# A sigmoid written as a tanh, and a new issue order, in a kernel of attention and a gated feed-forward layer

## The chip, the core and the metric

The kernel runs on one core of a Trainium2 chip. The metric is the device time of one execution in microseconds (us); lower is better. The engines are named as the profile names them: PE multiplies matrices (PEld is its weight load), ACT evaluates functions and copies, DVE does elementwise work and sums, POOL helps DVE and issues some transfers, SP issues most transfers. On-chip data lie in SBUF, results of PE in banks of PSUM.

## The reference

```python
# attention: 8 batches, 8 heads, 576 tokens, head size 64; keys and values are averaged over groups of 8 tokens
scores = q @ k_pooled.T / sqrt(64);  attn = softmax(scores);  x = attn @ v_pooled     # x becomes 4608 x 512
gate = 1.0 / (1.0 + np.exp(-(x @ w_gate)))                                           # w_gate 512 x 1536
out  = (gate * (x @ w_val)) @ w_out                                                  # w_out 1536 x 512
```

Everything is in 32-bit floats. The softmax needs `exp`, the gate a sigmoid.

## The kernel before

The tokens are handled in nine blocks of 512. Block 0 goes through `first_pass`, together with the preparation of blocks 1 and 2; then come four rounds of two blocks each (`hidden`, which computes the hidden values, and `second_sums`, which multiplies them by `w_out`). In a round the attention of the next two blocks is computed piece by piece between the products of the feed-forward layer.

To keep 32-bit precision, each operand of the large products is split into a high and a low part, and a product is three matmuls (high by high, high by low, low by high). The high part is a CAST on ACT, the low part a subtraction on DVE (in `first_pass` now and then on POOL). The rounds use sums and differences of quarters of the matrices, so that seven products do the work of eight; `sG`, `sV`, `s`, `y` in the profile are such partial results. The weights arrive as 64-bit numbers and are converted in `to_f32` with a `Prelu` and a `Relu` on ACT; the converted parts are kept in DRAM and loaded again in each round.

Three places compute the gate: `gate`/`h_of` in `first_pass`, `gated` at the start of the first round, and the end of `product` in the rounds. Each takes a 128x512 result of PE, applies the sigmoid on ACT, and multiplies it on DVE by the matching result of `w_val`. There are 108 such pairs of instructions. `attention`, `exps` and `total` compute the softmax; its sums are multiplied by `POOL` = 8 before the reciprocal is taken, which divides by the group size too.

The order in which instructions stand on their engines is not that of the code. The code runs once with `book.open`, and every instruction becomes a numbered unit; some matmuls that belong together are one unit. The string `LATER` lists all these numbers, and at the end the units are issued in its order:

```python
    with tc.manual_schedule(engines={e.engine for e in engines}):
        for n in LATER.split() or range(len(book.units)):
            for taken in book.units[int(n)]:
                taken.issue(link)
```

Each engine then works through its own instructions strictly in this order, and waits where an operand or a buffer isn't ready. ACT holds one table of functions at a time: where `Exp` follows `Sigmoid` or the other way round, the build puts an ACT_TABLE_LOAD in between; `Prelu`, `Relu` and copies need none.

All instructions are recorded by one helper, so the profile shows L317 for nearly all of them (L312 in the change, which has five lines fewer); the rows are told apart by the names of the tiles. `chain` are results of x by `w_gate` or `w_val`, `acc` results of the hidden values by `w_out`, `sc` scores, `tp` and `tr` transposed probabilities, `av` the attention's result, `xo` and `hs` split operands that stream through PE, `parts` and `oparts` split weights, `h` and `early` the hidden values and small data of the first pass that lie in the same room.

Of the kernel before, what the change touches and what calls it, by code (L numbers as in the profile page):

```python
# [15 lines left out]
AF = mybir.ActivationFunctionType  # L16
ALU = mybir.AluOpType
# [4 lines left out]
POOL = 8  # L22
# [7 lines left out]
BT = 512  # L30
# [299 lines left out]
def attention_then_ffn(ctx: ExitStack, tc: tile.TileContext, qT, kT, vm, vr, vn, sums8, wgv, wo, const, out, outT):  # L330
# [530 lines left out]


    bank, seen, gates, hb = {}, {}, {}, {}

    def chain_bank(kind, b):
        return ps.tile([P, BT], F32, name="chain", tag=CHAIN["GV".index(kind) * 3 + "ABC".index(b)])

# [710 lines left out]
```

## Time and profile before

| | |
|---|---|
| time, median of 3 runs | 905.96 us (905.59 to 908.38) |
| span of the profiled execution | 904.9 us |
| PE busy | 893.7 us, 99% |
| DVE busy | 657.9 us, 73% |
| ACT busy | 544.4 us, 60% |
| POOL busy | 199.5 us, 22% |
| ACT_TABLE_LOAD after the first | 47.5 us in 37 instructions |
| granted PE clock | 0.999 of full speed |

The profiled execution is not one of the three timed ones, and no time of its own is given beside its span; the median of the timed runs lies 1.06 us above the span. A matmul of 512 columns is recorded with about 392 ns, but the next one starts before it ends, so the busy time of PE is the union of such rows. Idle time of PE is what a change can give back; idle time of the others only matters where PE waits for them.

### The profile page before, as it was taken

Reading aid. Unit: us, or ns where it says so; the run is one execution under the profiler, and the core shown is the slowest. Engines: PE = TensorE matmul, PEld = TensorE weight load, DVE = VectorE, ACT = ScalarE, POOL = GpSimd, SP = SyncE. Lnnn points to the kernel's source line nnn. Section 1 sums busy time; section 2 is a strip of 40 time slices with the busy share of each in tenths; the row PEclk is TensorE's granted clock in tenths of the full one; section 3 lists DMA queues with packets and bytes.
Section 4 is the critical chain, followed back from the end, with each engine's and each line's share of the span. In section 5 each row is a group of like instructions: output and inputs, shape, how many; then the busy total and the mean of one; then the engine's idle time right before and its main releaser. Section 6 shows DMA issues by size and latency. Waiting matters only on the chain.

```text
span 904.9 us, 12649 instructions
## 1 busy us (share of the span) xinstructions
PE 893.7 (99%) x4162; PEld 734.5 (81%) x4162; DVE 657.9 (73%) x1039; ACT 544.4 (60%) x1108; POOL 199.5 (22%) x369
## 2 busy tenths in 40 slices
PE   7999999999999999999999999999999999999998
PEld 6778888888888888888888888888888888888886
DVE  7989888889899999756668796355589552224863
ACT  5998998788978476545375555445365552224352
POOL 2411101012164235453443104132213000000000
PEclk9999999999999999999999999999999999999999
DMA  9899888889999888798987888776747775646653
GB/s 344 289 329 340 304 338 294 297 290 333 319 334 305 282 288 286 233 302 257 308 278 233 245 274 259 235 265 196 266 120 254 244 251 206 228 166 206 195 167 141
DMA packets 100289, 237.56 MB, mean 263 GB/s; under 512 B 13856, under 2 KB 34720, under 8 KB 98688
## 3 DMA queue, kind: packets, MB, share of 16 engines
q1 hardware_dynamic: 85040, 203.84, 66.7%
q0 software_dynamic: 15040, 32.79, 10.7%
q8 instruction: 33, 0.54, 0.2%
q14 instruction: 32, 0.26, 0.1%
q10 hardware_dynamic: 144, 0.13, 0.0%
HBM read 176.02 MB, written 60.69 MB: 262 GB/s over the span
## 4 chain that ended last, share of the span: by engine, by line
PE 81%; ACT 2%; DVE 2%; issue 0%; DVEq 0%
PE chain L317 50%; PE acc L317 25%; PE av L317 3%; PE sc L317 3%; ACT hs L317 0%; DVE s L317 0%; DVE hs L317 0%; PE tp L317 0%; DVE h L317 0%; ACT e L317 0%; ACT L317 0%; ACT raw_o L317 0%; DVE w_o L317 0%; ACT w_o L317 0%; ACT oparts L317 0%
## 5 line engine op out<-in xcount | busy, mean ns | idle before, releaser
L317 PE MATMUL chain<-xo,parts 128*128 128x512 f32 x2316 | 544.0, 392 | 0.2 <-ACT xs L317 0.2
L317 PEld LDWEIGHTS chain<-xo,parts 128*128 128x128 f32 x2316 | 430.6, 188 | 93.0 <-issue 1.0
L317 PE MATMUL acc<-hs,oparts 128*128 128x512 f32 x1008 | 237.0, 391 | 0.3 <-issue 0.2
L317 PEld LDWEIGHTS acc<-hs,oparts 128*128 128x128 f32 x1008 | 188.1, 188 | 40.6 <-DVE hs L317 1.2
L317 POOL DMA_DIRECT2D turned<-turn x240 | 131.7, 551 | 215.9 <-DVE turn L317 184.4
L317 DVE TENSOR_TENSOR y<-chain,sV 128x512 f32<-128x512 f32 x46 | 31.2, 687 | 70.4 <-PE chain L317 54.7
L317 DVE TENSOR_TENSOR hs<-h,hs 128x1024 fp32r<-128x1024 f32 x52 | 63.0, 1218 | 10.5 <-ACT hs L317 10.3
L317 ACT CAST hs<-h 128x1024 fp32r<-128x1024 f32 x52 | 54.3, 1050 | 27.1 <-PE acc L317 22.3
L317 ACT COPY chain<-chain 128x512 f32<-128x512 f32 x46 | 26.4, 577 | 51.9 <-PE chain L317 42.5
L317 DVE TENSOR_TENSOR y<-chain,sG 128x512 f32<-128x512 f32 x46 | 31.3, 683 | 34.2 <-PE chain L317 23.5
L317 ACT CAST hs<-s 128x1024 fp32r<-128x1024 f32 x36 | 37.5, 1050 | 28.5 <-DVE s L317 13.0
L317 DVE TENSOR_TENSOR hs<-s,hs 128x1024 fp32r<-128x1024 f32 x36 | 43.8, 1219 | 11.1 <-ACT hs L317 10.8
L317 ACT COPY sG<-chain 128x512 f32<-128x512 f32 x46 | 26.6, 584 | 41.0 <-PE chain L317 39.3
L317 ACT ACT_TABLE_LOAD x37 | 47.5, 1283 | 0.6
L317 ACT COPY sV<-chain 128x512 f32<-128x512 f32 x46 | 26.7, 584 | 34.2 <-PE chain L317 32.9
L317 ACT ACTIVATE gate<-chain 128x512 f32<-128x512 f32 x46 | 26.9, 594 | 31.8 <-PE chain L317 29.0
L317 DVE TENSOR_TENSOR h<-chain,gate 128x512 f32<-128x512 f32 x46 | 30.8, 680 | 20.1 <-PE chain L317 20.0
L317 PE MATMUL sc<-kbd,raw 128*128 128x144 f32 (+1 forms) x262 | 41.3, 296 | 0.2 <-ACT pr L317 0.2
L317 PEld LDWEIGHTS sc<-kbd,raw 128*128 128x128 f32 (+1 forms) x262 | 33.5, 176 | 8.4 <-issue 2.8
L317 PE MATMUL acc<-oparts,hs 128*128 128x512 f32 x144 | 39.0, 403 | 0.4 <-DVE oparts L317 0.3
L317 ACT ACTIVATE gate<-y 128x512 f32<-128x512 f32 x46 | 28.9, 632 | 16.5 <-DVE y L317 16.4
L317 DVE TENSOR_REDUCE m<-sc 128x4 f32<-128x288 f32 x48 | 21.7, 453 | 17.5 <-PE sc L317 17.1
(212 smaller groups left out, 1104.5 us busy)
## 6 DMA issues: line engine op xcount, KB each, us to landing
oparts<-keptS SPq DMA_DIRECT2D x48, 512.0 KB, 4.3
oparts<-keptO SPq DMA_DIRECT2D x72, 256.0 KB, 4.2
raw<-in_wgv SPq DMA_DIRECT2D x12, 1024.0 KB, 8.7
out<-o SPq DMA_DIRECT2D x35, 256.0 KB, 3.5
raw<-in_kT SPq DMA_DIRECT2D x28, 288.0 KB, 5.0
raw<-in_qT SPq DMA_DIRECT2D x29, 256.0 KB, 5.1
raw<-in_vm SPq DMA_DIRECT2D x24, 256.0 KB, 5.7
raw_o<-in_wo SPq DMA_DIRECT2D x12, 512.0 KB, 9.1
```

The costliest lines, as they stand in the source:

```text
L317: return self._book.take(lambda: f(*args, **named))
```

## The change

The sigmoid is replaced through sigmoid(g) * v = (1 + tanh(g / 2)) * (v / 2). The halving is done at no instruction's cost: the softmax sums are multiplied by 16 instead of 8, so x and with it both products are half as large. The DVE multiplication becomes one SCALAR_TENSOR_TENSOR that adds 1 and multiplies. `Tanh` and `Exp` are in one table here: the built program has one ACT_TABLE_LOAD where that of before has 38. All other instructions are the same in kind and number (3967 matmuls, 1039 instructions of DVE, 555 transfers issued by SP). `LATER` is a new list; it no longer keeps exponentials and gates in groups.

```diff
 LATER = """
-6 5 4 7 0 11 3 2 21 8 25 27 19 28 14 18 23 31 22 20 9 26 13 35 17 36 33 1 10 40 45 76 39 37 12 48 47 52 16 55 32 66 38
...
-        nc.vector.tensor_scalar(out=zs, in0=zs, scalar1=EPS, scalar2=float(POOL), op0=ALU.add, op1=ALU.mult)
+        nc.vector.tensor_scalar(out=zs, in0=zs, scalar1=EPS, scalar2=2.0 * POOL, op0=ALU.add, op1=ALU.mult)
...
+    def gate_by(out, t, half):
+
+        nc.vector.scalar_tensor_tensor(out=out, in0=t, scalar=1.0, in1=half, op0=ALU.add, op1=ALU.mult)
...
-            nc.scalar.activation(gates[q[0]][:, q[1]], y, AF.Sigmoid)
+            nc.scalar.activation(gates[q[0]][:, q[1]], y, AF.Tanh)
...
-            nc.vector.tensor_tensor(
-                out=hb[f // 4][:, f % 4, q[0] * BT:(q[0] + 1) * BT], in0=y, in1=gates[q[0]][:, q[1]], op=ALU.mult
-            )
+            gate_by(hb[f // 4][:, f % 4, q[0] * BT:(q[0] + 1) * BT], gates[q[0]][:, q[1]], y)
...
-            nc.scalar.activation(ygate[f], vbank[0, f], AF.Sigmoid)
+            nc.scalar.activation(ygate[f], vbank[0, f], AF.Tanh)
...
-            nc.vector.tensor_tensor(out=h_at(f)[:, 0], in0=vbank[1, f], in1=ygate[f], op=ALU.mult)
+            gate_by(h_at(f)[:, 0], ygate[f], vbank[1, f])
```

`gated` and `total` change in the same way. What the new list does is seen in the engines' rows at three places.

**Place 1**, DVE at the very start (block 0). `e` and `early` are exponentials, `pm_226` and `early_217` (128x512) the probabilities of heads that PE transposes next, `rest` a remainder of keys. DVE before, first the step for the first heads, then that for the others:

```order
L317 TENSOR_TENSOR rest_251<-e_222,early_218 128x128
L317 TENSOR_TENSOR early_217<-e_222,early_218 128x512
L317 TENSOR_TENSOR pm_226<-e_222,early_218 128x512
...
L317 TENSOR_SCALAR early_218<-early_218 128x16
L317 TENSOR_TENSOR vres0_104<-vr_249,vres0_104 32x128
L317 RECIPROCAL early_218<-early_218 128x16
L317 TENSOR_TENSOR rest_261<-early_217,early_218 128x128
L317 TENSOR_TENSOR early_218<-early_217,early_218 128x512
```

DVE in the change, the same two steps:

```order
L312 TENSOR_TENSOR pm_226<-e_222,early_218 128x512
L312 TENSOR_TENSOR early_217<-e_222,early_218 128x512
...
L312 TENSOR_SCALAR early_218<-early_218 128x16
L312 RECIPROCAL early_218<-early_218 128x16
L312 TENSOR_TENSOR early_218<-early_217,early_218 128x512
L312 TENSOR_TENSOR rest_261<-early_217,early_218 128x128
```

The 128x512 products that PE waits for now stand ahead of `rest` and of `vres0`.

**Place 2**, ACT just after, at the first gates (`y`) and the exponentials of block 1 (`e_222` from `sc`). Before:

```order
L317 ACTIVATE raw64_239<-raw64_239,cst_84 128x1024
L317 ACTIVATE e_222,early_218<-sc_289,early_218 128x72
L317 ACT_TABLE_LOAD
L317 ACTIVATE y_285<-chain_281 128x512
L317 CAST parts_278<-w4_272 128x2x256
L317 CAST parts_280<-w4_272 128x2x256
L317 ACTIVATE y_282<-chain_277 128x512
L317 ACT_TABLE_LOAD
L317 ACTIVATE e_222,early_218<-sc_287,early_218 128x72
```

In the change:

```order
L312 ACTIVATE raw64_239<-raw64_239,cst_84 128x1024
L312 ACTIVATE y_282<-chain_277 128x512
L312 ACTIVATE e_222,early_218<-sc_289,early_218 128x72
L312 ACTIVATE e_222,early_218<-sc_287,early_218 128x72
L312 CAST parts_280<-w4_272 128x2x256
L312 ACTIVATE e_222,early_218<-sc_289,early_218 128x72
L312 ACTIVATE y_285<-chain_281 128x512
L312 ACTIVATE e_222,early_218<-sc_287,early_218 128x72 x3
```

The two loads are gone, and gates and exponentials alternate.

**Place 3**, PE at the first products with `w_out` (`acc`, from the split weights `oparts_301` and the split hidden values `hs_292`). Before:

```order
L317 MATMUL tr_309<-identr_85,r3_305 96x128 x4
L317 MATMUL chain_312<-xo1_269,parts_306 128x512 x6
L317 MATMUL chain_312<-xo2_274,parts_306 128x512 x6
L317 MATMUL acc_318<-oparts_301,hs_292 128x512
L317 MATMUL acc_316<-oparts_301,hs_292 128x512
L317 MATMUL acc_318<-oparts_301,hs_292 128x512
```

In the change:

```order
L312 MATMUL acc_318<-oparts_301,hs_292 128x512
L312 MATMUL chain_302<-xo2_274,parts_299 128x512 x6
L312 MATMUL tp_314<-cst_84,pm_226 128x128
L312 MATMUL tp_313<-cst_84,early_217 128x128 x2
L312 MATMUL tr_309<-identr_85,r3_305 96x128
L312 MATMUL chain_312<-xo1_269,parts_306 128x512 x6
L312 MATMUL tr_309<-identr_85,r3_305 96x128 x3
L312 MATMUL chain_312<-xo2_274,parts_306 128x512 x6
L312 MATMUL acc_319<-oparts_301,hs_292 128x512
```

The first `acc` matmul, which needs high parts alone, moved up, and small matmuls stand between the large ones in shorter groups. Such returns from a group of small matmuls to one of 512 columns are 84 in the order of before and 115 in that of the change.

## Rows read from the trace of the kernel before

**Rows 1.** Page, part 1: engine, busy us, share of the span, instructions.

```profile
PE 893.7 (99%) x4162; PEld 734.5 (81%) x4162; DVE 657.9 (73%) x1039; ACT 544.4 (60%) x1108; POOL 199.5 (22%) x369
```

**Rows 2.** Stretches: us, busy PE, PEld, DVE, ACT, POOL, clock, DMA.

```profile
28.00:140.00 112.00, 110.82 (x541) 90.36 (x540) 96.80 (x160) 105.56 (x254) 19.14 (x29) 1.00 0.89 321
140.00:360.00 220.00, 219.73 (x1054) 180.75 (x1053) 202.75 (x351) 167.38 (x396) 66.98 (x122) 1.00 0.88 302
360.00:660.00 300.00, 300.00 (x1396) 248.45 (x1395) 200.06 (x323) 152.66 (x277) 93.33 (x170) 1.00 0.78 254
```

**Rows 3.** Waits of PE: who for whom, us in total, times, longest.

```profile
PE tp L317 <- DVE r L317: 0.6, 1, 0.6
...
PE acc L317 <- DVE oparts L317: 0.3, 1, 0.3
PE tp L317 <- ACT y L317: 0.3, 1, 0.3
...
PE acc L317 <- issue: 0.2, 1, 0.2
```

**Rows 4.** Page, part 5: busy us, mean ns; idle before.

```profile
L317 PE MATMUL chain<-xo,parts 128*128 128x512 f32 x2316 | 544.0, 392 | 0.2 <-ACT xs L317 0.2
...
L317 ACT ACT_TABLE_LOAD x37 | 47.5, 1283 | 0.6
```

**Rows 5.** Timeline of ACT at place 2: start, us, what.

```profile
33.62 1.28 ACT L317 ACT_TABLE_LOAD   x1
34.91 0.60 ACT L317 ACTIVATE y<-chain 128x512 f32<-128x512 f32 x1
```

**Rows 6.** Timeline of ACT ahead of the wait of `tp` for `y`.

```profile
120.43 1.28 ACT L317 ACT_TABLE_LOAD   x1
...
123.24 0.60 ACT L317 ACTIVATE y<-chain 128x512 f32<-128x512 f32 x1
```

**Rows 7.** DVE by line and shape: busy us, mean ns.

```profile
L317 DVE TENSOR_TENSOR hs<-h,hs 128x1024 fp32r<-128x1024 f32 x52 | 63.0, 1218 | 10.5 <-ACT hs L317 10.3
...
L317 DVE TENSOR_TENSOR h<-chain,gate 128x512 f32<-128x512 f32 x46 | 30.8, 680 | 20.1 <-PE chain L317 20.0
...
L317 DVE SCALAR_TENSOR_TENSOR w<-w,raw 128x1024 uint32<-128x1024 uint32 x12 | 15.0, 1253 | 1.6 <-ACT raw L317 1.5
```

**Rows 8.** Timeline of DVE at place 1.

```profile
14.19 0.28 DVE L317 TENSOR_TENSOR rest<-e,early 128x128 f32<-128x128 f32 x1
...
20.00 0.69 DVE L317 TENSOR_TENSOR early<-early 128x512 f32<-128x512 f32 x1
```

**Rows 9.** Timeline of PE in the first 28 us.

```profile
15.13 0.55 PE L317 MATMUL tp<-cst,early 128*128 128x128 f32 x3 [0.92 <-DVE early L317]
...
27.69 2.52 PE L317 MATMUL chain<-xo,parts 128*128 128x512 f32 x10
```

**Rows 10.** Timelines of ACT and PE, 222 to 226 us.

```profile
222.64 1.28 ACT L317 ACT_TABLE_LOAD   x1
...
224.97 0.27 PE L317 MATMUL av<-pr,vres 96*128 96x192 f32 x1
225.31 0.76 PE L317 MATMUL sc<-kbd,raw 128*128 128x144 f32 x4
```

**Rows 11.** Chain that ended last, at 451 us: start, us, what.

```profile
451.20 0.49 PE sc L317 x4
...
453.07 0.49 PE sc L317 x4
```

**Rows 12.** The end: ACT and DVE timeline, then DMA issues (KB, us to landing).

```profile
900.77 0.37 ACT L317 COPY o<-acc 128x256 f32<-128x256 f32 x1 [0.77 <-PE acc L317]
...
901.24 0.42 DVE L317 COPY o<-acc 128x256 f32<-128x256 f32 x1 [6.09 <-ACT o L317]
...
out<-o SPq DMA_DIRECT2D x3, 256.0 KB, 2.0
...
out<-o SPq DMA_DIRECT2D x1, 128.0 KB, 1.7
```

More of the change, by code (lines that the diff above doesn't have):

```diff
@@ L931, in gated @@
         gate = two.tile([P, BT], F32, name="y", tag="y")
-        nc.scalar.activation(gate, whole("G", f, side), AF.Sigmoid)
-        nc.vector.tensor_tensor(
-            out=hb[f // 4][:, f % 4, side * BT:(side + 1) * BT], in0=whole("V", f, side), in1=gate, op=ALU.mult
-        )
+        nc.scalar.activation(gate, whole("G", f, side), AF.Tanh)
+        gate_by(hb[f // 4][:, f % 4, side * BT:(side + 1) * BT], gate, whole("V", f, side))
     EARLY = NP - 1
@@ L1275, in total @@
             zs = totals[j, g]
-            nc.vector.tensor_scalar(out=zs, in0=zs, scalar1=EPS, scalar2=float(POOL), op0=ALU.add, op1=ALU.mult)
+            nc.vector.tensor_scalar(out=zs, in0=zs, scalar1=EPS, scalar2=2.0 * POOL, op0=ALU.add, op1=ALU.mult)
             nc.vector.reciprocal(out=rz[j, g], in_=zs)
```

304 rows, old and new, of the table LATER are left out of this document.

## The prediction

> **What bounds the kernel now.** I read the page first. PE is busy 99% of the span, 893.7 of 904.9 us [rows 1], so PE idles for 11.2 us in all, and a change that leaves its instructions alone can't give back more. The stretches come next. From 360 to 660 us PE is busy 300.00 of 300.00 us at a granted clock of 1.00, the full 2.4 GHz, while ACT is busy about half of it. From 28 to 140 us, the first pass, PE is still busy 110.82 of 112.00 us, but ACT is at 105.56 and DVE at 96.80: only here is ACT short of time [rows 2]. The waits of PE say who is late. After the start that view has six, from 0.3 us (for the low part of `oparts`; for a gate `y`) down to 0.2 us, 1.4 us together [rows 3]. The rest of the idle time is the start (27.69 us pass before the first large product [rows 9]) and the end.
>
> A wait costs more than its gap. One matmul is recorded with 392 ns, but 2316 of them fill 544.0 us, 235 ns each [rows 4]: in steady flow each overlaps the next by 0.16 us, and a wait loses that overlap too. Six waits then cost 1.4 + 6 x 0.16 = 2.4 us. For waits too short for that view I add 0.5 us, an estimate: one of them is at 225.31, where PE starts the scores 0.07 us after the end of its last matmul [rows 10], which makes 0.07 + 0.16 = 0.23 us, and I assume another. Removable after the start: 2.9 us at most.
>
> **Table loads.** 37 loads go, at 1283 ns 47.5 us of ACT's time [rows 4]. None stands on PE's path for its length. After the load at 33.62 the gate begins at 34.91 us, 1.29 us later [rows 5], and PE runs on meanwhile. What the 1.28 us can do is seen where PE does wait behind one: the load at 120.43 us pushes two gates back, the second ends at 123.84 [rows 6], and a transposition that needs its PSUM bank waits 0.3 us for it [rows 3]. Without the load that wait is gone: 0.3 + 0.16 = 0.46 us. The same goes for the exponentials behind the load at 222.64, for which the scores at 225.31 wait: 0.23 us.
>
> The Trainium skill, "ScalarE: Activation LUTs", section "What ACT_TABLE_LOAD costs", states 1283 ns for the load and about 1380 ns of DRAIN more, 2.66 us a switch. The first figure agrees with the row; the second doesn't show here, since 1.29 us separate a load's start from the next gate's. By the page ACT would get back 37 x 2.66 = 98 us in place of 47.5 (an estimate), and the sum for PE would stay, capped by PE's waits.
>
> **Tanh for sigmoid, and the DVE instruction.** No row shows Tanh. There are 108 gates; were each 0.1 us longer, 10.8 us of the 47.5 would be used up, and were each as much shorter, ACT would gain as much more; I take no difference. The fused DVE instruction isn't in the trace on these operands either. From below: the plain product takes 680 ns for 512 columns. From above: the same kind of fused instruction on 1024 columns of integers takes 1253 ns where a plain one takes 1218 [rows 7], 3% more, which would be 0.02 us here and 108 x 0.02 = 2.2 us of DVE. I take 0. The halving rides on a constant and costs nothing.
>
> **The start.** Until 14.19 us DVE has the same work in both orders. Then the 128x512 products come ahead of `rest`, which takes 0.28 us [rows 8], and PE, which started its transpositions at 15.13 [rows 9], starts some 0.2 us sooner. In the second step the order moves `vres` and a `rest` behind the product that stood at 20.00 us [rows 8]: two such small ones, 0.5 us, where PE waited 0.6 us [rows 3]. PE is then nearly full until 27.69, so I let the large products begin 0.5 us sooner. Bounds: 0, because a sum of keys and two small subtractions now stand ahead of the low part of `xo` in DVE's rows, and DVE may be the later one; and 0.7 us, if both steps count in full.
>
> **Place 3.** Before, PE waits there 0.3 us for the low part of `oparts` [rows 3]. ACT makes its high part after three loads fewer, 3.85 us, and one cast fewer. DVE, which makes the low part, has four more small instructions ahead of it (counted in the order), at some 0.3 us each [rows 8], 1.2 us. PE reaches the seventh `acc` matmul, the first that needs the low part, after as many large matmuls as before, and 0.5 us sooner by the start. So the wait becomes a little shorter or stays: I credit half of 0.3 + 0.16, 0.23 us.
>
> **The other waits.** What is left of the 2.9 us is 2.9 - 0.46 - 0.23 - 0.46 = 1.75 us. They aren't behind a load directly, but the list is new and ACT has slack in the first pass: 7 of the 37 loads, 9.0 us, lie between 28 and 140 us, more than the 6.4 us that ACT idles there (112.00 - 105.56) [rows 2]. I credit half, 0.87 us.
>
> **What the new order adds.** Small matmuls stand in shorter groups, with 31 more returns to large ones. The same four score matmuls take 0.49 us behind `av` and between large products alike [rows 11], so a return costs nothing that shows; from above I allow 0.05 us each, 1.5 us, and take 0.3. New waits can't be read from an order: I put 0.3 us, against the 2.9 us that the list of before leaves.
>
> **The end.** The last two products are swapped. Before, half a bank is copied by ACT and the other half by DVE after it, until 901.66, 0.9 us after the ACT copy starts, and 128 KB take 1.7 us to land. Now a full bank is copied by ACT, about 0.6 us, and 256 KB take 2.0 us [rows 12]. 0.9 + 1.7 against 0.6 + 2.0 us: no change.
>
> **The sum.** 0.46 + 0.23 + 0.5 + 0.23 + 0.87 - 0.3 - 0.3 = 1.7 us. The profiled span of 904.9 becomes 903.2; the runs' median lies 1.06 above the span, so 904.3 us, 0.19% less. A measurement of this kernel can tell about 0.3%, 2.7 us, from no change, so the forecast is that no difference can be told.
>
> **Rivals.**
>
> *The loads are hidden anyway.* The 47.5 us lie beside a PE that is full, old waits come back at other places, and the start is bound by DVE's low part of `xo`. For it: 14 of the loads lie after 360 us, where PE hardly waits. Against: two waits stand directly behind loads. Time 905.9 us, also no difference.
>
> *All waits go.* With ACT no longer short in the first pass, a list can be found in which PE hardly waits: 2.9 us, and 0.7 at the start, 3.6 less, 902.4 us. For it: what makes that stretch tight, ACT at 94%, is just what is relieved. Against: DVE is at 86% there and gets nothing back, and at place 3 it is DVE that is late.
>
> *DVE falls behind.* If the fused instruction is twice as slow with an operand in PSUM, each gate costs 0.68 us more of DVE. In the first pass there are 12, 8.2 us, against 15.2 us that DVE idles there; from 140 to 360 us it idles only 17.2 us (220.00 - 202.75), and a round has up to 24 gates, 16.3 us [rows 2, 7]. If half of the idle time can be filled, PE begins to pay one to one at 7.6 us in the first pass and at 8.6 us in the second stretch: 0.6 and some 7 us, part of which later slack takes back; I put 909.5 us. For it: no row has the instruction on PSUM. Against: the plain product with a PSUM operand costs 680 ns where half of one with 1024 columns from SBUF is 609, so PSUM isn't slow as such.
>
> That the loads stay is excluded: the built program has one.
>
> **Chances.** Forecast (903.3 to 905.3) 0.45; hidden anyway (905.3 to 908) 0.22; all waits go 0.20; DVE behind 0.13. Faster by over 0.3% (under 903.2) is the third, 0.20; within it the first two, 0.67; slower (over 908.7) the last, 0.13. The range leaves out the slower case and the best half of the faster one: 902.4 to 907.5 us.
>
> **What would show it.** Right: ACT busy near 497 us, DVE near 658, fused rows near 680 ns; the first large product at about 27.2 us; no wait of PE for `y`; PE's waits after the start under 1 us together. Wrong: fused rows over 0.8 us, or PE waiting over 0.5 us for DVE at a time (slower); the first large product before 26.5 us, or a PE busy time that falls although its matmuls are the same in number (faster), since the 392 ns rows would then hide waits that I count as work.

## The result, and the profile after

The change makes the kernel slower: 913.3 us median (908.5 to 915.2, 8 executions) against 907.1 (905.6 to 908.4, 8 executions), ratio 1.0059 [1.0044, 1.0074]. I had forecast 904.3; my range ended at 907.5, and the slowest time that I put on a rival was 909.5. The profiled execution took 915.2 us, its span is 913.4; it is the slowest of the eight.

The page first, then stretches (us, busy PE, PEld, DVE, ACT, POOL, clock, DMA), the last two chosen for their clock:

```profile
PE 898.9 (98%) x4162; PEld 739.4 (81%) x4162; DVE 660.6 (72%) x1039; ACT 497.6 (54%) x1071; POOL 210.2 (23%) x369
```

```profile
28.00:140.00 112.00, 111.10 (x549) 91.14 (x548) 100.45 (x166) 98.56 (x249) 27.52 (x31) 1.00 0.89 321
140.00:360.00 220.00, 217.44 (x1042) 178.39 (x1041) 198.49 (x340) 143.63 (x372) 68.17 (x118) 1.00 0.89 300
360.00:660.00 300.00, 296.97 (x1365) 244.71 (x1364) 201.45 (x324) 135.00 (x261) 94.17 (x172) 0.99 0.77 253
369.20:372.60 3.40, 3.40 (x9) 2.61 (x9) 3.01 (x6) 0.00 (x0) 3.15 (x7) 0.50 0.55 162
10.80:17.60 6.80, 6.80 (x29) 6.23 (x29) 5.65 (x15) 2.45 (x8) 0.00 (x0) 0.50 1.05 414
```

ACT lost 46.8 us of work [rows 1], as it was to. PE is still the bound, but it idles 14.5 us where it idled 11.2, and not in the first pass: there it is busy 111.10 of 112 us, a little more than before [rows 2]. The holes are behind 140 us, where PE had been full. The last two rows show a granted clock of 0.50, that is 1.2 GHz in place of 2.4, for 6.8 us near the start and 3.4 us at 369 us. At half the clock work of 3.4 and of 1.7 us takes twice as long. These 5.1 us are nearly all of the 5.2 by which PE's busy time grew, for the same 4162 matmuls (both pages have that number, not the 3967 given above). So of the 8.5 us by which the span grew, 3.3 are idle time and the rest is busy time at half the clock.

Waits of PE (who for whom, us in total, times, longest), then the group of DVE's waits that matters:

```profile
PE chain L312 <- DVE xo L312: 2.3, 1, 2.3
PE sc L312 <- DMA h<-in_qT: 1.7, 2, 1.5
...
PE sc L312 <- ACT e L312: 1.6, 2, 1.3
PE acc L312 <- DVE r L312: 0.9, 1, 0.9
PE acc L312 <- DMA oparts<-keptO: 0.8, 1, 0.8
...
PE chain L312 <- DMA parts<-keptV3A: 0.3, 1, 0.3
```

```profile
DVE turn L312 <- DMA turned<-turn: 15.2, 5, 4.6
```

In the kernel before that last group had 4.2 us in 3 waits, the longest 2.1. No wait for a gate `y` of the kind in [rows 3] is left, but two rows behind the start name a transfer (`oparts<-keptO`, `parts<-keptV3A`), where before PE waited for none there, and the wait for `h<-in_qT` at the start had 0.7 us. Three places show where the waits come from.

**369 us.** DVE, with its idle time and what ended it, then PE:

```profile
362.90 0.44 DVE L312 TENSOR_REDUCE m<-sc 128x4 f32<-128x288 f32 x1
367.10 0.71 DVE L312 STREAM_TRANSPOSE turn<-pm 128x512 f32<-128x512 f32 x1 [3.76 <-DMA turned<-turn]
367.74 1.18 DVE L312 TENSOR_TENSOR xo<-s,xo 128x1024 fp32r<-128x1024 f32 x1
```

```profile
368.97 4.38 PE L312 MATMUL chain<-xo,parts 128*128 128x512 f32 x11 [2.32 <-DVE xo L312]
```

`turned` transposes the probabilities in two steps: DVE transposes 32x32 blocks into `turn`, and transfers on POOL's queue place them in DRAM, twelve of them ahead of this row. There is one room for `turn`, so the next `turn<-pm` must wait until these have landed. Nothing needs this `turn` soon; what PE needs is the low part of `xo` one row further. The engine that waits is DVE, the one that pays is PE. In the order of before the same row stands behind the `xo` rows and waits for nothing.

The chain that ended last gives the transfer that DVE waited for (start, us, what):

```profile
361.87 5.01 DMA turned<-turn
...
367.10 0.06 DVE turn L312
```

**209 us.** The same view, at the wait of `sc` for `e`:

```profile
199.46 0.42 SPq L312
199.88 0.04 issue
199.93 7.98 DMA raw<-in_vr
...
208.04 0.69 DVE vs L312
...
208.81 0.14 ACT vrc L312
...
208.96 0.41 ACT e L312 x2
...
209.42 0.76 PE sc L312 x4
```

ACT and PE there:

```profile
208.81 0.24 ACT L312 CAST vrc<-vs 96x64 fp32r<-96x64 f32 x1 [3.02 <-DVE vs L312]
...
209.42 0.76 PE L312 MATMUL sc<-kbd,raw 128*128 128x144 f32 x4 [1.25 <-ACT e L312]
```

SP issues a 64 KB load at 199.93 us, behind loads of `w` and `raw<-in_qT` for later work; it lands 8 us later. DVE and ACT wait for it in turn, and the exponentials that free PE's bank stand on ACT behind the copy `vrc`. ACT is idle for 3.02 us ahead of it: the loads of tables are gone, and ACT waits for data instead.

**The start.** PE's timeline:

```profile
10.59 2.05 PE L312 MATMUL sc<-kbd,h 128*128 128x144 f32 x8 [1.47 <-DMA h<-in_qT]
12.57 2.02 PE L312 MATMUL vr<-xs 64*96 64x128 f32 x8
...
29.67 0.71 PE L312 MATMUL chain<-xo,parts 128*128 128x512 f32 x2
```

The third load of q is issued behind `xs<-in_vn`, at 4.64 us where it was at 4.02. PE waits, then runs at 1.2 GHz, and the first large product begins at 29.67 us, 1.98 us later than in [rows 9]. The order alone does not make it that late. e3 and e6 (below) have the same loads at the start and waits of 1.3 and 1.5 us for that load, but in their profiles the clock stays at 1.00 up to 28 us, and the product begins 0.54 and 0.41 us later than before. e13 and e14 have the load ahead again, and yet a slow stretch, of 6.8 and 3.4 us, and begin 1.55 and 1.62 us later. So some 0.5 us belong to the order and the rest to a slow stretch that one execution has and another has not.

To see where time goes, compare when the same product begins. There are 3468 matmuls of 512 columns in `chain` and `acc`; the table gives how much later than before the n-th of them begins, in profiled executions, worked out from the start times of PE's rows (us; the experiments are below). One execution stands for each kernel; those of the change and of e14 are 1.9 and 3.0 us slower than their medians.

| n | before at | after | e1 | e5 | e10 | e14 |
|---|---|---|---|---|---|---|
| 1 | 27.7 | +1.98 | -0.36 | -0.49 | -0.51 | +1.62 |
| 441 | 154.8 | +0.46 | -0.60 | -0.93 | -0.15 | +0.06 |
| 1161 | 342.0 | +2.87 | -1.47 | -1.45 | -1.02 | +0.48 |
| 1281 | 371.6 | +8.14 | -1.46 | -1.45 | +3.31 | +1.53 |
| 1641 | 462.0 | +9.84 | -1.49 | +3.40 | +11.72 | +3.96 |
| 3468 | 900.3 | +8.86 | -1.59 | +2.60 | +11.62 | +4.64 |

The late start is nearly made up by 155 us. Then 2.4 us go up to 342, 5.3 up to 372 (the wait of 2.32, 1.7 for the clock, the rest in smaller pieces), 1.7 more up to 462, and nothing behind it.

### The profile page after: what moved, and what is told of

Its sections match the earlier page's. It is cut to its first block, busy times and chain, and to the rows that moved or that the text cites. A ratio compares the mean times of both kernels' runs of the same rounds, so it can differ in the third digit from the quotient of the medians.

```text
span 913.4 us, 12630 instructions
## 1 busy us (share of the span) xinstructions
PE 898.9 (98%) x4162; PEld 739.4 (81%) x4162; DVE 660.6 (72%) x1039; ACT 497.6 (54%) x1071; POOL 210.2 (23%) x369
## 4 chain that ended last, share of the span: by engine, by line
PE 78%; DMA 6%; DVE 4%; POOL 3%; issue 2%; ACT 1%; SPq 1%; DVEq 0%; POOLq 0%; ACTq 0%
PE chain L312 44%; PE acc L312 27%; PE av L312 3%; PE sc L312 3%; POOL turned L312 2%; DMA turned<-turn 2%; DMA raw<-in_vr 1%; DMA oparts<-keptO 1%; DMA parts<-keptV3A 1%; SPq L312 1%; DMA w<-keptWO 1%; PE tp L312 1%; DVE h L312 0%; DVE y L312 0%; DVE turn L312 0%
## 5 line engine op out<-in xcount | busy, mean ns | idle before, releaser
L312 PE MATMUL chain<-xo,parts 128*128 128x512 f32 x2316 | 549.6, 393 | 3.2 <-DVE xo L312 2.3
L312 DVE SCALAR_TENSOR_TENSOR h<-gate,chain 128x512 f32<-128x512 f32 x46 | 31.0, 680 | 23.9 <-PE chain L312 21.6
L312 DVE SCALAR_TENSOR_TENSOR h<-gate,y 128x512 f32<-128x512 f32 x46 | 31.3, 683 | 14.3 <-ACT gate L312 13.7
```

The lines of the kernel that those rows point to most:

```text
L312: return self._book.take(lambda: f(*args, **named))
```

## Experiments

Each was timed in five rounds beside the kernel before on the same chip. Where only the list differs, all use the new arithmetic (tanh), unless said otherwise. "Old" and "new" are the two lists.

**Arithmetic or list.** e1 is the changed kernel with the old list; e4 the kernel before with the new list. The first line of the list in the change and in e1:

```diff
 LATER = """
-6 2 21 27 4 28 35 5 19 7 26 11 0 3 18 8 9 13 14 31 39 25 20 23 17 22 36 66 10 40 45 52 1 33 32 67 48 53 12 62 58 76 38
+6 5 4 7 0 11 3 2 21 8 25 27 19 28 14 18 23 31 22 20 9 26 13 35 17 36 33 1 10 40 45 76 39 37 12 48 47 52 16 55 32 66 38
...
```

> The change's arithmetic (tanh, fused gate, one table load) with the list of before. If the new list is what costs time, this is 903.5 to 907 us, no slower than before; the 37 loads come off ACT and the waits behind loads at 120 and 222 us go. If the gates or a faster ACT cost the time, it is 911 us or more, like the change.

> The kernel of before (sigmoid, plain product) with the new list; the build puts in 56 table loads, 18 more than before and 55 more than the change, 71 us of ACT. If loads are hidden beside PE: within 2 us of the change, 911 to 915 us. If the freed time of ACT is what the new list lives on: 918 us or more. If the tanh arithmetic is what costs the time: under 908 us.

e1: 905.84 us, 0.9988 [0.9979, 0.9997]. e4: 951.02 us, 1.0486 [1.0462, 1.0510]. So with the old list the arithmetic gains some 0.1%, and the whole loss is in the list. e4 shows that the new list needs the arithmetic: without groups it has 56 loads, and PE waits for exponentials (its table loads, then PE's first wait):

```profile
L312 ACT ACT_TABLE_LOAD x55 | 70.6, 1283 | 1.4 <-PE chain L312 0.6
```

```profile
PE sc L312 <- ACT e L312: 10.5, 7, 3.4
```

The loads take 70.6 us of ACT, and e4 is some 38 us slower than the change, which has the same list without them (44 slower than before). The Trainium skill, "ScalarE: Activation LUTs", section "What ACT_TABLE_LOAD costs", states 2.66 us a switch; the row has 1283 ns again, with 1.4 us of idle time ahead of all 55 together, so the rest of the 2.66 does not show here.

**Which part of the list.** e2: old up to 140 us, then new. e3: the reverse. e5: old up to 372 us, then new. e8: old up to 28 us, new up to 140, old behind it. The line of each list where the first seam is, in the order e2, e3, e5, e8:

```diff
+810 872 855 865 838 856 822 848 849 809 689 743 735 750 792 839 866 867 815 857 858 813 814 812 833 870 836 859 873 843
...
+809 833 870 811 953 806 772 807 817 957 816 818 851 852 853 828 854 872 855 865 838 856 822 848 849 819 842 879 850 880
...
+2050 1988 2113 1994 1990 2051 2115 1992 2114 1964 2052 2119 2158 2122 2053 1965 2176 1977 2006 2108 2116 2007 1982 2002
...
+140 162 150 167 149 165 127 163 157 217 164 151 147 168 159 190 171 57 160 50 56 161 170 231 169 245 175 166 172 173
```

> The change with the list of before for the first 842 units (up to 140 us) and the new order for all others. If the rounds of the new list hold the loss (a transposition on DVE that waits for a transfer ahead of the operand that PE needs at 369 us, and late loads), this is 910 to 914 us. If the late third q load at the start and the low clock behind it are the cause, it is 905 to 907 us.

> The counterpart: the new list for its first 837 units (up to 140 us), the order of before for all others. If the rounds hold the loss: 905 to 908 us, since the new first pass begins 2.0 us late and has made up 1.5 us of it by 150 us. If the start holds it: 911 us or more.

> The changed kernel (tanh) with the old list's order up to its row at 372 us and the new list's order behind it. Theory: the new list loses its time between 140 and 372 us alone, where rows that wait for late transfers stand ahead of operands of PE. Then this is as the old list with tanh, 905.0 to 907.0 us. Rival: the new list loses in all rounds, behind 372 us too, where the changed kernel's profile shows PE waiting 0.45 and 0.27 us: then 908 us or more.

> The changed kernel (tanh) with a list of three parts: the old order up to 28 us, the new order up to 140 us, the old order behind it. Theory: the new list's start loses about 0.9 us against the old list with tanh, its order from 28 to 140 us gains about 1.6 us, so both good parts together gain more than either kernel tried so far: 904.0 to 905.3 us, 0.9965 to 0.998 of before. Rival: what the new order gained from 28 to 140 us was only the start's loss made up again, since later work waits for the same transfers either way: 905.5 to 906.3 us as with the two lists tried.

e2: 913.76 us, 1.0070 [1.0043, 1.0097], as slow as the change. e3: 906.16, 0.9984 [0.9976, 0.9993], as good as e1. So the first pass of the new list, bad start and all, costs nothing; its rounds cost everything. e5: 909.41, 1.0028 [1.0016, 1.0040]. My theory put the whole loss ahead of 372 us and fell: part of it lies behind. e8: 905.87, 0.9984 [0.9976, 0.9993]. Here too the rival's range holds the time: the good start of the one list and the good middle of the other don't add up to a gain that shows, though the interval still reaches the 0.998 at which the theory's range ended.

**Single places.** e6 moves the `turn<-pm` of 369 us behind the `xo` rows; e7 adds three moves of loads.

```diff
 L312 TENSOR_REDUCE m<-sc 128x4
-L312 STREAM_TRANSPOSE turn<-pm 128x512
 L312 TENSOR_TENSOR xo_828<-s,xo_828 128x1024
 L312 TENSOR_REDUCE ks<-raw 128x72
...
 L312 TENSOR_TENSOR e<-sc,m 128x288
+L312 STREAM_TRANSPOSE turn<-pm 128x512
```

> The changed kernel with one unit moved: VectorE's transposition turn<-pm, for which PE waited 2.32 us at 368.97 us, stands ten DVE rows later, behind the xo rows, as in the old list. Theory: PE's wait goes, and with it the stretch at 1.2 GHz behind it (about 1.6 us), in the executions that have them: 909.5 to 911.5 us in the median, the highest runs below 914. Rival: the late transfer only holds up the next row instead, or the loss is spread over many rows: 912 to 914 us.

> The changed kernel with four moves: the one of turn<-pm behind the xo rows, the three loads of raw<-in_vr (PE's wait of 1.25 us at 209.42) ahead of the load that SyncE's queue was held by, two loads oparts<-keptO (wait of 0.76 us at 290.66) ahead of the load that held them up, and the third load of q at the start ahead of xs<-in_vn (wait of 1.47 us at 10.59, then 1.2 GHz up to 17.63). Theory: these places are the loss. Regained are 3.9 + 1.25 + 0.76 us and 1.5 to 2 us at the start, 7.4 to 7.9 us, so 906 to 909 us with something left for waits that move. Rival: the order as a whole is worse, and each wait comes back at the next late row: 911 us or more.

e6: 912.23 us, 1.0056 [1.0037, 1.0074], e7: 910.56, 1.0041 [1.0029, 1.0053]. e6 lies in its rival's range, e7 between its two. In e6's profile the wait at 369 us and its slow stretch are gone, yet the time hardly moves: PE now waits at later places, 0.76 us at 397 and 1.6 us at 446, both behind other `turn<-pm` rows (idle 3.89 and 4.16 us ahead of them, at 392.24 and 444.21). In e7 the load moved ahead of `h<-keptwG` made that one late: DVE waited 3.93 us for it, and PE 1.3 us at 204.75. One place was not the cause; the kind of row might be.

**The kind of row.** e10 is the test from the other side: the old list, which has no such trouble, with four `turn<-pm` moved ahead. One of the four:

```diff
 L312 SCALAR_TENSOR_TENSOR h<-gate_870,y 128x512
+L312 TENSOR_TENSOR pm<-e,rz 128x512
+L312 STREAM_TRANSPOSE turn<-pm 128x512
 L312 TENSOR_TENSOR vrc<-vs,vrc 32x64
 L312 TENSOR_TENSOR s_936<-w_935,s_936 128x256
 L312 TENSOR_REDUCE vs<-raw 128x64
 L312 TENSOR_TENSOR y<-chain,sG_949 128x512
-L312 TENSOR_TENSOR pm<-e,rz 128x512
 L312 TENSOR_TENSOR y<-chain,sV_967 128x512
-L312 STREAM_TRANSPOSE turn<-pm 128x512
```

> The old list with tanh (905.8 us), with four rows turn<-pm moved ahead as the new list has them: by six DVE rows (the one at 364.4 us), six rows with its pm row (393.1), four with its pm row (438.7) and seven (452.5). Nothing else differs. Theory: each then waits on VectorE for the transfers of the turn before it, and PE for the VectorE rows behind it; 2 to 5 us more, 907.5 to 911 us. Rival: the place of these rows does not matter, since the transfers end in time in the old list: 905.3 to 906.5 us.

e10: 918.04 us, 1.0115 [1.0100, 1.0130]: 12 us for four rows moved by four to seven places (two with their `pm` row), more than I expected. DVE, PE and a stretch behind it:

```profile
387.14 0.68 DVE L312 TENSOR_TENSOR pm<-e,rz 128x512 f32<-128x512 f32 x1
397.00 0.71 DVE L312 STREAM_TRANSPOSE turn<-pm 128x512 f32<-128x512 f32 x1 [9.19 <-DMA pt<-turned]
```

```profile
399.67 1.65 PE L312 MATMUL chain<-xo,parts 128*128 128x512 f32 x3 [3.44 <-DVE y L312]
```

```profile
399.70:405.20 5.50, 5.50 (x13) 4.34 (x14) 1.97 (x3) 1.59 (x4) 4.50 (x9) 0.51 0.91 279
```

The row names `pt<-turned`, which stands behind the transfers `turned<-turn` on the same queue; it lands at 397.35, when the row has already begun, and the last of the twelve `turned<-turn` lands at 396.88, so these are what DVE waited for. DVE stands still for 9 us, PE for 3.4, and then PE runs at 1.2 GHz for 5.5 us. The waits of PE that e1 doesn't have are 3.4, 2.5, 1.1 and 0.8 us, with 0.16 us of lost overlap each; the slow stretches, 5.5 us at 0.51 and 4.6 us at 0.63 behind 363.2, add some 4.4. That makes 12.8 us, against 12.7 by which e10 falls back between products 1161 and 1641.

The Trainium skill, "DMA: Bandwidth & Descriptors", section "Rules for kernel authors", advises to issue a transfer early, compute, and wait for it late. e10 agrees: the same transfers, waited for some rows sooner, cost 12 us. The same skill's "TensorE: Matmul & The Clock Gate", section "What's actually happening", says that the throttled clock is the default and activity lifts it; rows of 0.50 and 0.51 behind PE's waits agree.

e12 is e5 with three `turn<-pm` rows moved back; e9 is e7 with four more of them moved back, and with the loads `raw<-in_vr` behind `h<-keptwG`, which they had made late. e12's first:

```diff
 L312 TENSOR_TENSOR pl<-pt,ph 128x512
-L312 STREAM_TRANSPOSE turn<-pm 128x512
 L312 TENSOR_TENSOR vrc<-vs,vrc 32x64
 L312 TENSOR_REDUCE vs<-raw 128x64
...
 L312 TENSOR_TENSOR sums<-s_936,sums 128x2x256
+L312 STREAM_TRANSPOSE turn<-pm 128x512
 L312 TENSOR_TENSOR pm<-e,rz 128x512
```

> The kernel that has the old order up to 372 us and the new one behind it (909.4 us), with three rows turn<-pm of its second part moved behind rows that don't need their transfer (at 392.42, 442.80 and 453.3 us of that kernel, by six, one and four DVE rows). Theory: PE's waits of 1.27 us at 396.92 and 0.89 us at 444.87 go, with 0.16 us each: 906.5 to 908 us. Rival: VectorE's late rows there have other causes, and nothing is regained: 909 to 910 us.

> The changed kernel with the four moves of the run before (the three loads of raw<-in_vr now behind the load h<-keptwG that VectorE needs, which had been late in that run), and four more of VectorE's rows turn<-pm moved behind rows that don't need their transfer: the ones at 262.60, 398.93, 448.62 and 459.57 us, by three, six, one and four DVE rows. Theory: the rows turn<-pm, each of which waits for the transfers of the turn before it, are most of what is left: 907 to 909.5 us. Rival: a turn that is moved back delays what needs it, and the waits move along: 910 to 911 us as with four moves.

e12: 908.36 us, 1.0007 [0.9997, 1.0016], from e5's 1.0028: three rows are worth 0.2%, half of what e5 loses against e1, though 908.36 lies just above the theory's range (before stood 0.8 us higher beside this set). e9: 910.22, 1.0026 [1.0014, 1.0038], above the 909.5 that my theory allowed and in the range of its rival, 910 to 911. Its profile has no PE wait behind a `turn` over 0.9 us, but two new ones for the `oparts` loads that I had moved, of 2.6 and 1.8 us, of which this is the first:

```profile
287.79 1.61 PE L312 MATMUL acc<-hs,oparts 128*128 128x512 f32 x5 [2.61 <-DMA oparts<-keptO]
```

e7 has the same moves and no such wait in its profile, so they need not make one. e14 below is e9 without them and comes out 0.2% lower, with intervals that overlap: that they cost time is likely, not shown.

**The start's loads.** e11 is e1 with SP's loads of the first 12 us in the new order.

```diff
 L312 DMA h<-in_kT 128x576
+L312 DMA xs_220<-in_vn 64x512
 L312 DMA h<-in_qT 128x512
+L312 DMA early<-in_vn 128x512 x2
+L312 DMA xs_220<-in_sums 128x360
 L312 DMA early<-in_qT 128x512
-L312 DMA xs_220<-in_sums 128x360
-L312 DMA xs_220<-in_vn 64x512
```

> The old list with tanh (905.8 us), where only the loads of the first 12 us on SyncE's queue stand in the new list's order: the third load of q behind xs<-in_vn, the first loads early<-in_vn ahead of xs<-in_sums and early<-in_qT. Theory: this order is the loss at the start, PE waits 1.3 to 1.5 us for h<-in_qT, and falls to 1.2 GHz behind it in some executions: 907.0 to 908.5 us. Rival: the time is made up in the first pass, where VectorE and ScalarE are the ones waited for: 905.3 to 906.5 us.

e11: 907.66 us, 0.9993 [0.9982, 1.0004], 0.0005 above e1 with intervals that overlap. Inconclusive: the median lies in the theory's range, but before stood 0.6 us higher beside this set than beside e1, and the two intervals allow at most 2.3 us (1.0004 less 0.9979), far from the loss.

**What is left.** e13: the new list with the five `turn<-pm` rows moved back and the third load of q ahead. e14: also the three loads of `raw<-in_vr` ahead of a load of `w`.

```diff
 L312 DMA h<-keptwG_176 128x1024
+L312 DMA raw<-in_vr 32x512 x3
 L312 DMA w_654<-keptwG_180 128x1024
-L312 DMA raw<-in_vr 32x512
 L312 DMA keptS_214<-sums 128x512
 L312 DMA raw<-in_qT 128x512
-L312 DMA raw<-in_vr 32x512
...
```

> The changed kernel with the five rows turn<-pm moved behind rows that don't need their transfers, and the third load of q ahead of xs<-in_vn; all other loads as in the new list. Theory: the turns are the larger part of the loss and the two moved loads oparts<-keptO of the run before cost what they were to save: 908 to 910 us, 1.001 to 1.0025 of before. Rival: the turns only hid late loads, which are now waited for: 911 us or more, 1.004.

> The same with the three loads of raw<-in_vr behind h<-keptwG and ahead of w<-keptwG, for which PE waited 1.25 us at 209.42. Theory: late loads are the rest, this one is worth 1.2 us: 907 to 908.8 us. Rival: PE's wait there moves to the next late row, and nothing is regained: within 0.5 us of the kernel without this move.

e13: 910.68 us, 1.0035 [1.0017, 1.0052]. It lies between the two expectations: the `turn` rows and the load of q together give back a third of what the list loses, with an interval that overlaps that of the change. e14: 908.23, 1.0006 [0.9989, 1.0023], in the theory's range: three small loads moved by a few places are worth another 0.3%, though the intervals still touch. That is more than the 1.25 us that PE waits for them in the profile of after; in e13's the same wait, at 210.02 us, is 2.1 us, and behind it the granted clock is 0.50 for 3.4 us, which costs 1.7 us more. What PE still waits for in e14:

```profile
PE acc L312 <- DMA oparts<-keptO: 1.7, 3, 0.7
...
PE chain L312 <- DMA parts<-keptV3A: 1.0, 1, 1.0
...
PE sc L312 <- DVE e L312: 0.8, 1, 0.8
```

With thirteen units moved the new list is back at before, and what remains is mostly of the same two kinds. Executions of e14 spread from 904.4 to 912.8 us, those of before beside it from 906.2 to 909.1. I read this as an order that waits for transfers and so takes over their scatter; no run shows it by itself. The clock is not the whole of it: e2 spreads from 910.1 to 918.8 us with mean clocks of 0.997 to 1.000. The fastest kernels of the study are e1, e3 and e8, 0.12 to 0.16% faster than before, all with the old rounds.

A second room for `turn`, which would take the wait away at its root, was not tried. Open stays how the remaining difference of e14 to e1, some 1.6 us, divides among its late loads.

## Why the prediction was wrong, point by point

- **The bound** was right in naming PE. That only its idle time counts was not: more than half of what the profiled span grew by is busy time at half the clock, which no term of the sum allowed for. And the cap was read one-sidedly: 11.2 us is what can be given back, but nothing caps what can be lost.
- **The base** rested on a small sample: 905.96 was the median of three runs, and eight gave 907.1. The 1.06 us between median and span was no offset either: the profiled execution of the change took 1.8 us more than its span. Against 907.1, the 0.19% that I forecast would be 905.4.
- **Table loads, tanh, fused instruction** were right. ACT 497.6 us (about 497 expected), DVE 660.6 (658), and the rows are as cheap as the old ones [rows 7]:

```profile
L312 DVE SCALAR_TENSOR_TENSOR h<-gate,chain 128x512 f32<-128x512 f32 x46 | 31.0, 680 | 23.9 <-PE chain L312 21.6
...
L312 DVE SCALAR_TENSOR_TENSOR h<-gate,y 128x512 f32<-128x512 f32 x46 | 31.3, 683 | 14.3 <-ACT gate L312 13.7
```

  A gain of the size worked out for loads shows too, where the list is left alone: e1's profiled span is 903.3 us, 1.6 less than before. Of the sum, 0.46 + 0.23 us belong to the loads by themselves, and e1's ratio of 0.9988 makes 1.1 us, with an interval from 0.3 to 1.9. The 0.46 us behind [rows 6] are in it: neither e1 nor after waits there.
- **The start** had the wrong sign: 0.5 us sooner was forecast, 1.98 later came, and 0.4 to 0.5 later in e3 and e6, where the clock held. I read DVE's rows and not SP's, where the third load of q had moved behind another. e3 and e11 show that this did not decide the result.
- **Place 3**: the wait for the low part of `oparts` went, one of 0.9 us for `r` came at 54.52. The 0.23 us credited was not there; e3 and e8, with the same order here, have that wait too.
- **The end** was right to 0.4 us: from the start of ACT's last copy to the end of the span it is 3.8 us, before 4.2 [rows 12].

```profile
909.63 0.59 ACT L312 COPY o<-acc 128x512 f32<-128x512 f32 x1 [0.99 <-PE acc L312]
```

- **The step that failed** is "New waits can't be read from an order: I put 0.3 us, against the 2.9 us that the list of before leaves." The new waits, with the slow stretches behind them, are worth 6.4 us in the ratios (1.0059 against e1's 0.9988), twenty times the term. PE's waits after the start, which I expected to be under 1 us together, are 6.5 us in the profile, where they were 1.4. An estimate from the waits of a well-ordered list says nothing about another list. And the order did show it: I compared it at three places in the first pass and at none behind 140 us, where PE was full and had only to lose, and I looked for late engines, not for rows that wait for transfers. The step "The other waits" leaned on the same belief that a new list is a better one. The 31 more returns to large matmuls, for which I took 0.3 us, no run separates; e14 has the same order on PE as the change, so they are part of its 1.6 us against e1 at most, as far as the intervals tell.
- **The rivals.** "DVE falls behind" had the right sign and the wrong mechanism: DVE is late not because its work is longer but because it stands still for transfers, 15.2 us in one group. "The loads are hidden anyway" holds for the old list to about 1 us (e1) and not at all for the new one (e4). "All waits go" came nowhere near. No rival was a badly placed wait, though the list was the larger part of the change.

## What to carry to other kernels

When a change brings a new order, cost the order by itself: for each row that waits for a transfer, look at what stands behind it on its engine and who needs that. A row whose result nobody needs soon belongs behind those that are needed, above all when it waits for a buffer with one room; and a small load belongs ahead of large ones that are needed later. Try new arithmetic and new order apart: here the first was worth 0.1% and the second cost 0.7%.

## What the runs showed of the hardware

- A wait of PE can cost nearly twice its length: behind the 2.32 us at 368.97 the granted clock was 0.50 for 3.4 us, behind 3.44 us in e10 it was 0.51 for 5.5 us. Not every wait does: behind the 1.25 us at 209.42 it stayed at 1.00. Not every execution has it either: over the eight executions of the change the mean clock runs from 0.994 to 1.000, and the one at 1.000 is the fastest, 908.5 us.
- The transfers `turned<-turn` were the limit of how soon `turn<-pm` rows can follow each other: in the change, with twelve of them between, a row that waited came 16.2 us after the one before (350.9 and 367.1 us), with eight 11.0 us (448.6 and 459.6). POOL took 0.55 us to issue one, and the last of the twelve took 5.01 us to land.
- A load of 64 KB took 7.98 us from issue to landing where many loads stood in the queue; the median of its group is 4.3.

```profile
raw<-in_vr SPq DMA_DIRECT2D x36, 64.0 KB, 4.3
```
